# First token mix from row classes of the strided heads, wide strided loads, early buffers in late weights' places

## The chip, the core and the metric

The kernel runs on one core of one Trainium2 chip. The time is device microseconds for one execution, from inputs in DRAM to the output in DRAM. It is given as the median of several runs; beside it stands one profiled execution, whose trace is read here. The engines of the core: PE (TensorE, matmuls; PEld is its weight load), DVE (VectorE), ACT (ScalarE), POOL (GpSimd), SP (SyncE, which here issues nearly all DMAs).

## What is computed

```python
# attention: q, k, v are [8, 8, 576, 64], scale 1/8
mask_local   = (rel >= 0) & (rel < 32)                      # heads 0..3
mask_strided = (rel >= 0) & (pos_k % 32 == pos_q % 32)      # heads 4..7
attn = softmax(where(mask, scale * q @ k.T, -1e9)); x = concat_heads(attn @ v)   # x: [8, 576, 512]
# token mix of rank 32, then an MLP with a residual
u  = x + (x.transpose(0, 2, 1) @ U @ V).transpose(0, 2, 1)  # U: [576, 32], V: [32, 576]
out = u + relu(u @ w_ch1) @ w_ch2                           # w_ch1: [512, 2048], w_ch2: [2048, 512]
```

The inputs U, V, w_ch1 and w_ch2 arrive as 64-bit floats, all others as 32-bit.

## The kernel before

The rows of x are cut into tiles of 128 (four per batch, and one shared tail per pair of batches), two tiles to a block, 18 blocks. Each block runs 16 steps, one for each 128 columns of w_ch1: GEMM1 (L706, 12 matmuls 128x256 into ph) gives h^T, ACT writes relu(h) rounded (gh, L710), DVE what is left of it (gl, L711), and GEMM2 (L723, 6 matmuls 128x512) adds to the block's accumulator. Three products (high by high, low by high, high by low) stand for one product in full 32-bit precision. u^T of a block is held as uh and ul in the same sense. Blocks 0 and 1 run interleaved, block 1 two steps behind.

The weights come as 32 chunks of 128x512 64-bit numbers, 512 KB each, in the order group g = 0..3, then w1 (i = 0) or w2 (i = 1), then t = 0..3; chunk number 8g + 4i + t. A chunk is loaded raw (L150) and turned into a rounded high and a low part in the same place: ACT takes the absolute value of the upper words into a buffer cv (L110, Abs), DVE shifts and joins three times (L112, L113, L115), ACT casts the high part (L168), POOL subtracts for the low part (L169). There are three cv buffers; one is held from Abs to the end of L169. Step fc of block 0 or 1 needs w1 chunks of its group g = fc // 4.

The strided heads of batches 0 and 1 run on PE (early_strided): k and q are read with 18 rows a head and 32 positions to a row (tile kq), transposed (L343), scored (L356), softmaxed in s_str, multiplied with v (tile sv, L388) into two halves o_str, and these go through DRAM (tile od) into the layout of x (tile xg; L401). Strided heads of the other batches run on POOL and DVE. Local heads (early_local and its blocks) run on PE, with vt as the values. The token mix of batch 0 first makes t = x^T U (mix_t_first, L553 to L567), then adds V^T t to x in place (mix_u, L576 to L584) and transposes blocks 0 and 1 in the middle of it (transposes, L671 to L676).

The program is written as generators that are drawn in a loop (first_attention, then the loop over steps); a scheduler then fixes the order on each engine. CONV0, CONVE say from which draw on, and how often, a chunk is converted before the steps begin; LD0, LDR when weights are loaded; B1S when batch 1's attention begins. SP's queue issues its DMAs in program order, and an issue waits until the eighth one before it has landed. The q loads of batch 0 go through ACT's queue.

Of the kernel before, what the change touches and what calls it, by code (L numbers as in the profile page):

```python
# [7 lines left out]
F32 = mybir.dt.float32  # L8
# [27 lines left out]

@with_exitstack
def fused_kernel(ctx, tc, q, k, v, U, V, w1_in, w2_in, masks, eye, out):
# [48 lines left out]

    last_dma = [None]

# [13 lines left out]
    def to_f32(raw, p, n):  # L103


        rv = raw.bitcast(I32).rearrange("p (n two) -> p n two", two=2)
        lo_w, hi_w = rv[:, 0:n, 0], rv[:, 0:n, 1]
        cv = cvt("cv")
        f = cv[0:p, 0:n]
        nc.scalar.activation(out=f, in_=hi_w.bitcast(F32), func=AF.Abs, scale=2.0 ** -112)  # L110
        i = cv.bitcast(I32)[0:p, 0:n]
        nc.vector.tensor_scalar(out=i, in0=i, scalar1=3, scalar2=None, op0=ALU.logical_shift_left)  # L112
        nc.vector.scalar_tensor_tensor(out=i, in0=hi_w, scalar=-0x80000000, in1=i,  # L113
                                       op0=ALU.bitwise_and, op1=ALU.bitwise_or)
        nc.vector.scalar_tensor_tensor(out=i, in0=lo_w, scalar=29, in1=i,  # L115
                                       op0=ALU.logical_shift_right, op1=ALU.bitwise_or)
        return f

    def small_weights():
# [197 lines left out]
    def early_strided(b, eng=None):  # L317


        tb = 64 * (b % 2)  # L320
        quarters = [slice(32 * h, 32 * h + NCH) for h in range(4)]
        kq = [[ubuf([128, 1024], "kq") for _ in range(2)] for _ in range(2)]
        for bufs in kq:
            for x, buf in enumerate(bufs):
                (nc.vector if b == 0 and x == 0 else nc.gpsimd).memset(buf, 0.0)
# [7 lines left out]
        for h in range(4):  # L333
            dma(out=sv[quarters[h]], in_=v[b, 4 + h].rearrange("(i r) d -> i (r d)", r=32))
        yield
# [24 lines left out]
        yield  # L360
        s_sb = ubuf([128, 1024], "s_str")
        nc.gpsimd.memset(s_sb, 0.0)
# [5 lines left out]
        yield  # L368
        nc.scalar.activation(out=sv4, in_=sv4, func=AF.Exp, scale=0.125)
        yield  # L370
# [7 lines left out]
        yield  # L378
        o_sb = [ubuf([128, 16, D], "o_str") for _ in range(2)]
        od = dp.tile([4, 32, 32, D], F32, name="od")  # L380
        nj = 4 * width
        for r0 in range(0, 32, 2 * nj):
# [14 lines left out]
            if r1 + 2 * nj == 16:  # L397
                dma(out=od.rearrange("h i r d -> (h i) r d")[:, 16 * half:16 * half + 16], in_=o_sb[half])
        yield
        xg, xt = x_tiles(b)  # L400
# [142 lines left out]

    def mix_t_first(b, tst):

        xg, xt = x_tiles(b)
        tb = 64 * (b % 2)
        ta = att([128, DM], "ta")
        for half in range(2):
            cs = slice(256 * half, 256 * half + 256)  # L550
            ps_a = psx1()[:, 0:256]
            for j in range(4):
                nc.tensor.matmul(ps_a[32 * j:32 * j + 32, :], U_sb[:, j, :], xg[:, j, cs], start=True, stop=False,  # L553
                                 skip_group_check=True, tile_position=(0, 32 * j))
            for j in range(4):
                part = slice(64 * j, 64 * j + 64)
                nc.tensor.matmul(ps_a[32 * j:32 * j + 32, part], U_sb[tb:tb + 64, 4, :],
                                 xt[tb:tb + 64, 256 * half + 64 * j:256 * half + 64 * j + 64], start=False, stop=True,
                                 skip_group_check=True, tile_position=(tb, 32 * j))
            nc.scalar.copy(out=ta[:, cs], in_=ps_a)  # L560
        yield
        st = psx2()
        for half in range(2):
            cs = slice(256 * half, 256 * half + 256)
            nc.tensor.matmul(st[0:96, half, 0:256], fold, ta[:, cs], start=True, stop=True)
            nc.scalar.copy(out=tst[:, cs], in_=st[0:96, half, 0:256])
            nc.vector.tensor_tensor(out=tst[32:64, cs], in0=st[32:64, half, 0:256], in1=tst[32:64, cs].bitcast(F32), op=ALU.subtract)  # L567
        yield

    def mix_u(b, tst):  # L570
        xg, xt = x_tiles(b)
        tb = 64 * (b % 2)
        for t in (0, 2):
            pv = psx2()
            for s in range(2):
                nc.tensor.matmul(pv[:, s, :], Vst[:, 128 * (t + s):128 * (t + s) + 128], tst, start=True, stop=True)  # L576
# [3 lines left out]
            if b == 0 and t < 2 * NLEAD:  # L580
                yield from transposes(t // 2)
        pv = psx1()
        nc.tensor.matmul(pv[0:tb + 64], Vst[:, 512 - tb:576], tst, start=True, stop=True)
        nc.vector.tensor_tensor(out=xt[tb:tb + 64, :], in0=pv[tb:tb + 64, :], in1=xt[tb:tb + 64, :], op=ALU.add)  # L584
        yield
# [12 lines left out]
    def mixed(b, halves_):  # L598
        tst = att([96, DM], "tst", F32R)
        if b == 0:  # L600
            yield from mix_t_first(b, tst)
        else:
            for half in halves_:
                yield from mix_t(b, tst, half)
        yield from mix_u(b, tst)

    def first_attention():
# [14 lines left out]
        sw = small_weights()  # L622
        next(sw)
        yield
# [4 lines left out]
        yield from mixed(b, (0, 1))  # L629

# [13 lines left out]

    vt0 = const.tile([128, 1184], F32, name="vt0")
    fold = ap_.tile([128, 336], F32, name="s_st", tag="s_st")[:, 0:96]

# [11 lines left out]
    def transposes(n):  # L659
# [5 lines left out]
        if n < N_PE_T:  # L665
            uh, ul = parts()
            pts = psx2()
            for s, tid in enumerate(blocks[n]):
                x = tile_src(tid)
                for dc in range(NDC):  # L670
                    nc.tensor.transpose(out=pts[:, s, 128 * dc:128 * dc + 128], in_=x[:, 128 * dc:128 * dc + 128],  # L671
                                        identity=ident)
                src = pts[:, s, :].rearrange("p (d a x) -> p d a x", d=NDC, x=32)
# [7 lines left out]
        for s, tid in enumerate(blocks[n]):  # L681
            x = tile_src(tid)
            nc.vector.transpose(out=bt[:, :, s].rearrange("p q d x -> p d q x"),
                                in_=x.rearrange("p (d q y) -> p d q y", q=4, y=32))
            yield
# [12 lines left out]
    def gemm1(n, fc):  # L698
# [10 lines left out]
        gl = mp.tile([128, 256], F32R, name="gl", bufs=3)  # L709
        nc.scalar.activation(out=gh[:, 0:W], in_=ph[:, 0:W], func=AF.Relu)  # L710
        nc.vector.scalar_tensor_tensor(out=gl[:, 0:W], in0=ph[:, 0:W], scalar=0.0, in1=gh[:, 0:W].bitcast(F32),  # L711
# [47 lines left out]
    for i, _ in enumerate(first_attention()):  # L759
        load_ahead(int((i - LD0) * LDR))  # L760
        if i >= CONV0 and i % CONVE == 0:
            convert(counts["conv"] + 1)
# [8 lines left out]
    sgen, sb, free = None, NSP, False  # L771
    tr = None
    seq = sorted(((n, fc) for n in range(NLEAD) for fc in range(NFC)), key=lambda z: (z[1] + SKEW * z[0], z[0]))
    seq += [(n, fc) for n in range(NLEAD, len(blocks)) for fc in range(NFC)]
    lead_t = seq.index((0, NFC - 1)) if NLEAD > 1 else NFC - 6
    for step, (n, fc) in enumerate(seq):
# [15 lines left out]
        if nb < B and step >= window[nb][0]:  # L792
# [5 lines left out]
            while done < want:  # L798
# [66 lines left out]
```

## Time and profile before

| | |
|---|---|
| median of 3 runs | 1039.06 us (1036.94 to 1039.64) |
| profiled execution | 1040.9 us |
| its span in the trace | 1039.0 us |
| mean granted clock of PE | 0.959 |
| DMA, whole span | 72.06 MB, mean 69 GB/s |

The span is what the trace covers; the profiled execution's time holds 1.9 us more. A page of the profile gives busy time by engine and groups of instructions; windows cut the span by time. How a row reads: start, length, engine, line, operation, output and inputs, shapes, count, and in brackets how long the engine was idle before it and what released it.

### The profile page before, as it was taken

The page shows a single profiled execution, that of the slowest core. Times are in us where ns is not written, and L with a number is a line of the kernel's source. Part 1 is how long each engine was busy: PE and PEld are TensorE (multiplying, and loading weights), DVE is VectorE, ACT ScalarE, POOL GpSimd, SP SyncE. Part 2 cuts the span into 40 slices and gives each one's busy share as a digit, 9 for nine tenths or more (in the row PEclk, how much of TensorE's full clock was granted, in tenths as well). Part 3 has the DMA queues.
Part 4 walks back from the last instruction along what each step waited for, and adds up shares of the span by engine and source line. Part 5 has one row for each costly group of instructions (what it writes and reads, how often), then busy time and mean ns, then how long its engine had stood idle before and what let it go on. Part 6 is the DMA issues. An engine that isn't in the chain of part 4 may idle for free.

```text
span 1039.0 us, 21886 instructions
## 1 busy us (share of the span) xinstructions
PE 966.9 (93%) x9056; PEld 832.6 (80%) x9056; DVE 610.7 (59%) x1117; ACT 273.2 (26%) x635; POOL 360.3 (35%) x389
## 2 busy tenths in 40 slices
PE   4535788999999999999999999999999999999997
PEld 3424576888888888888888888888888888999996
DVE  1727798577767674761657875786587754222121
ACT  2414454212421242111332133213321332211110
POOL 2122254645284434640319341944194400000000
PEclk9556799999999999999999999999999999999999
DMA  6576742414323224131240434043404300101000
GB/s 147 145 163 170 254 190 45 74 48 83 60 53 69 62 47 66 27 81 39 49 73 19 88 64 89 4 95 57 87 10 94 53 21 13 50 1 41 1 21 21
DMA packets 182571, 72.06 MB, mean 69 GB/s; under 512 B 156856, under 2 KB 172504, under 8 KB 182328
## 3 DMA queue, kind: packets, MB, share of 16 engines
q1 hardware_dynamic: 181056, 69.78, 29.4%
q8 instruction: 71, 1.16, 0.5%
q10 hardware_dynamic: 1416, 0.89, 0.3%
q14 instruction: 28, 0.23, 0.1%
HBM read 51.22 MB, written 11.53 MB: 60 GB/s over the span
## 4 chain that ended last, share of the span: by engine, by line
PE 83%; DVE 7%; DMA 6%; issue 2%; SPq 2%; ACT 0%; DVEq 0%; ACTq 0%
PE ph L706 38%; PE acc L723 36%; DMA raw<-in_moe_w_ch_dram 3%; DVE cv L115 2%; SPq L94 2%; PE px L723 1%; PE px L223 1%; DVE cv L113 1%; DVE st L498 1%; PE px L255 1%; PE px L527 1%; PE px L243 1%; DMA kq<-in_k_dram 1%; PE px L576 1%; PE px L531 1%
## 5 line engine op out<-in xcount | busy, mean ns | idle before, releaser
L706 PE MATMUL ph<-uh,w 128*128 128x256 f32 x2304 | 468.3, 286 | 7.4 <-DVE gl L711 7.4
L706 PEld LDWEIGHTS ph<-uh,w 128*128 128x128 f32 x2304 | 375.1, 189 | 25.3 <-DVE gl L711 11.1
L723 PE MATMUL acc<-w,gh 128*128 128x512 f32 x1088 | 350.6, 401 | 5.5 <-ACT gh L710 5.4
L706 PE MATMUL ph<-ul,w 128*128 128x256 f32 x1152 | 326.1, 283 | 0.0
L711 DVE SCALAR_TENSOR_TENSOR gl<-ph,gh 128x256 fp32r<-128x256 f32 x288 | 121.0, 420 | 289.3 <-ACT gh L710 288.1
L710 ACT ACTIVATE gh<-ph 128x256 fp32r<-128x256 f32 x288 | 110.1, 383 | 520.0 <-PE ph L706 470.9
L706 PEld LDWEIGHTS ph<-ul,w 128*128 128x128 f32 x1152 | 218.2, 189 | 10.5
L723 PEld LDWEIGHTS acc<-w,gh 128*128 128x128 f32 x1088 | 193.5, 189 | 39.8 <-ACT gh L710 5.6
L723 PE MATMUL acc<-w,gl 128*128 128x512 f32 x544 | 215.8, 397 | 0.0
L468 POOL TENSOR_TENSOR tmp<-st 128x576 f32<-128x576 f32 (+6 forms) x162 | 166.9, 1067 | 133.9 <-DMA vt<-in_v_dram 85.5
L496 POOL TENSOR_TENSOR tmp<-st,s_st 128x448 f32<-128x448 f32 (+7 forms) x162 | 136.1, 869 | 214.2 <-DVE st L498 84.4
L498 DVE TENSOR_REDUCE st<-tmp 128x64 f32<-128x64 f32 (+8 forms) x162 | 135.9, 866 | 2.5 <-POOL tmp L496 1.7
L723 PEld LDWEIGHTS acc<-w,gl 128*128 128x128 f32 x544 | 102.4, 188 | 20.5
L470 DVE TENSOR_REDUCE s_st<-tmp 128x9 f32<-128x576 f32 (+6 forms) x162 | 87.5, 563 | 15.7 <-POOL tmp L468 15.6
L169 POOL TENSOR_TENSOR w<-cv,w 128x512 fp32r<-128x512 f32 x32 | 44.9, 1406 | 119.9 <-ACT w L168 119.9
L112 DVE TENSOR_SCALAR cv<-cv 128x512 int32<-128x512 int32 (+3 forms) x35 | 23.3, 667 | 51.7 <-ACT cv L110 51.6
L513 ACT COPY xg<-st 32x256 f32<-32x256 f32 x96 | 38.8, 404 | 23.5 <-DVE st L498 22.5
L115 DVE SCALAR_TENSOR_TENSOR cv<-raw,cv 128x512 int32<-128x512 int32 x32 | 34.0, 1063 | 0.5
L110 ACT ACTIVATE cv<-raw 128x512 f32<-128x512 f32 x32 | 21.8, 680 | 36.4 <-DMA raw<-in_moe_w_ch_dram 27.7
L693 DVE TENSOR_TENSOR ul<-u,uh 128x1024 fp32r<-128x1024 f32 x15 | 18.4, 1229 | 20.6 <-ACT uh L692 14.7
L168 ACT CAST w<-cv 128x512 fp32r<-128x512 f32 x32 | 19.9, 621 | 33.3 <-DVE cv L115 29.3
L343 PE MATMUL ph<-ident,kq 128*128 128x128 f32 x64 | 15.0, 398 | 14.0 <-DMA kq<-in_k_dram 9.8
(127 smaller groups left out, 603.5 us busy)
## 6 DMA issues: line engine op xcount, KB each, us to landing
raw<-in_moe_w_ch_dram SPq DMA_DIRECT2D x32, 512.0 KB
out_dram<-xg SPq DMA_DIRECT2D x32, 256.0 KB
u<-bt SPq DMA_DIRECT2D x240, 32.0 KB
vt<-in_v_dram SPq DMA_DIRECT2D x32, 144.0 KB
vt<-in_v_dram SPq DMA_DIRECT2D x32, 136.0 KB
st<-in_q_dram SPq DMA_DIRECT2D x24, 144.0 KB
st<-in_k_dram SPq DMA_DIRECT2D x24, 144.0 KB
st<-in_v_dram SPq DMA_DIRECT2D x24, 144.0 KB
```

The source lines that it names most:

```text
L112: nc.vector.tensor_scalar(out=i, in0=i, scalar1=3, scalar2=None, op0=ALU.logical_shift_left)
L115: nc.vector.scalar_tensor_tensor(out=i, in0=lo_w, scalar=29, in1=i, op0=ALU.logical_shift_right, op1=ALU.bitwise_or)
L169: nc.gpsimd.tensor_tensor(out=lo, in0=f, in1=hi.bitcast(F32), op=ALU.subtract)
L468: nc.gpsimd.tensor_tensor(out=tmp[:, 0:n], in0=sk[:, j0:j0 + n], in1=sq[:, i:i + 1].broadcast_to([128, n, D]), op=ALU.mult)
L470: late.append(lambda tmp=tmp, n=n, i=i, j0=j0: nc.vector.tensor_reduce(out=s_st[:, i, j0:j0 + n], in_=tmp[:, 0:n], axis=AX.X, op=ALU.add))
L496: nc.gpsimd.tensor_tensor(out=tv, in0=sv[:, 0:i + 1, d0:d0 + step], in1=s_st[:, i, 0:i + 1].broadcast_to([128, i + 1, step]), op=ALU.mult)
L498: late.append(lambda tv=tv, i=i, d0=d0, step=step: nc.vector.tensor_reduce(out=o_st[:, i, d0:d0 + step], in_=tv.rearrange("p j d -> p d j" ...
L513: nc.scalar.copy(out=xg[32 * i4:32 * i4 + 32, :, cs], in_=o_st[rows, i4:16:4, :])
L706: nc.tensor.matmul(ph[:, 0:W], w_parts[0, g, dc][:, part, fs], ut[:, :, :, dc, :], start=(dc == 0 and i == 0), stop=(dc == NDC - 1 and i = ...
L710: nc.scalar.activation(out=gh[:, 0:W], in_=ph[:, 0:W], func=AF.Relu)
L711: nc.vector.scalar_tensor_tensor(out=gl[:, 0:W], in0=ph[:, 0:W], scalar=0.0, in1=gh[:, 0:W].bitcast(F32), op0=ALU.max, op1=ALU.subtract)
L723: nc.tensor.matmul(accs[n][:, s, :], gt[:, cs], w_parts[1, g, f][:, part, :], start=(fc == 0 and i == 0), stop=(fc == NFC - 1 and i == 2))
```

## The change

**Loads.** k, q and v of the four strided heads come in one DMA each, from 32 rows a head instead of 18 (the last 14 rows of a head read into what follows it in memory and are not used); the memsets of kq go. The w1 chunks with t of 2 or 3 are loaded with rows permuted in the same manner.

**Places.** kq, s_str, o_str and three new tiles take the places of late weight chunks (28 to 31; 22 and 27; 20, 21 and 26, 24; 23 to 25) in place of the pool "u".

**First mix.** t of the strided half is made from o_str itself: U is written to DRAM (ud) and read back by row class (U_cls), 128 matmuls (32 classes, 4 heads) give its part of t, and u^T of blocks 0 and 1 is x^T, by matmuls with ident, plus t^T V in the same PSUM tile (first_u). mix_u of batch 0 follows behind step 4. The columns of the upper half of x are kept permuted, which splits a transpose or a product in two at several places.

**Conversions.** Abs (L112 of the changed kernel) is issued behind the exp of the strided heads, or behind the latest gh. Nine chunks are converted ahead of the steps, and batch 1's attention begins six draws later.

```diff
-LD0, LDR = 4, 0.5
+LD0, LDR = 8, 0.5
+MU0 = 4
-CONV0, CONVE = 12, 3
-B1S, B1E = 16, 1
+CONV0, CONVE, CONVP = 11, 1, 9
+B1S, B1E = 22, 1
...
-        nc.scalar.activation(out=f, in_=hi_w.bitcast(F32), func=AF.Abs, scale=2.0 ** -112)
+        with tc.issue_after(gate[0]) if gate else nullcontext():
+            nc.scalar.activation(out=f, in_=hi_w.bitcast(F32), func=AF.Abs, scale=2.0 ** -112)
...
+        ud = dp.tile([S, R], F32, name="ud")
+        dma(out=ud[0:512].rearrange("(t p) r -> p t r", p=128), in_=U_sb[:, 0:4])
+        dma(out=ud[512:576], in_=U_sb[0:64, 4])
+        for h in range(4):
+            dma(out=U_cls[32 * h:32 * h + NCH], in_=ud.rearrange("(i r) k -> i (r k)", r=32))
...
-                w1_in[128 * t:128 * t + 128, 512 * g:512 * g + 512]
+                w1_in[128 * t:128 * t + 128, 512 * g:512 * g + 512] if t < 2 else \
+                bass.AP(w1_in.tensor, w1_in[256 + 32 * (t - 2):, 512 * g:512 * g + 512].offset, [[64 * FF, 4], [FF, 32], [1, 512]])
...
+    def late(x, shape, name, dtype=F32):
+
+        i, g, t = chunks[x]
+        return const.tile(shape, dtype, name=name, tag=f"w{i}_{g}_{t}")
...
+        def wide(src, n, a):
+
+            return bass.AP(src.tensor, src[b, 4:5].offset + a, [[S * D, 4], [32 * D, 32], [1, n]])
+
+        kq = [[late(28 + 2 * x + y, [128, 1024], "kq") for y in range(2)] for x in range(2)]
...
-                for h in range(4):
-                    dma(out=bufs[half][quarters[h]],
-                        in_=src[b, 4 + h].rearrange("(i r) d -> i (r d)", r=32)[:, 1024 * half:1024 * half + 1024], eng=e)
+                dma(out=bufs[half], in_=wide(src, 1024, 1024 * half), eng=e)
...
-            dma(out=sv[quarters[h]], in_=v[b, 4 + h].rearrange("(i r) d -> i (r d)", r=32))
+        dma(out=sv, in_=wide(v, 32 * D, 0))
...
-        s_sb = ubuf([128, 1024], "s_str")
+        s_sb = late(22 if b == 0 else 27, [128, 1024], "s_str")
...
-        o_sb = [ubuf([128, 16, D], "o_str") for _ in range(2)]
+        o_sb = [late(x, [128, 16, D], "o_str") for x in ((20, 21) if b == 0 else (26, 24))]
...
+    def mix_first(tst):
...
+        for r in range(32):
+            for h in range(4):
+                rows = slice(32 * h, 32 * h + NCH)
+                nc.tensor.matmul(ps_b[32 * h:32 * h + 32], U_cls[rows, R * r:R * r + R], o_cls[r // 16][rows, r % 16],
+                                 start=r == 0, stop=r == 31, skip_group_check=True, tile_position=(32 * h, 32 * h))
...
+    def first_u(n, tst):
...
+        for d in range(4):
+            nc.tensor.matmul(pu[:, d // 2, 256 * (d % 2):256 * (d % 2) + 256], tst[:, 128 * d:128 * d + 128], Vst[:, 256 * n:256 * n + 256],
+                             start=False, stop=True, skip_group_check=True)
+        for a in range(2):
+            src = pu[:, a].rearrange("p (d s x) -> p d s x", d=2, x=32)
+            gate[:] = [nc.scalar.copy(out=uh[:, 2 * a:2 * a + 2], in_=src).ins]
+            nc.vector.tensor_tensor(out=ul[:, 2 * a:2 * a + 2], in0=src, in1=uh[:, 2 * a:2 * a + 2].bitcast(F32), op=ALU.subtract)
+        yield
...
+        yield from mix_first(tst0)
+        fu = [first_u(n, tst0) for n in range(NLEAD)]
...
+        if step >= MU0 and mu is not None and next(mu, "end") == "end":
+            mu = None
```

How the order on three engines moves. Line numbers of the changed kernel differ: L95 and L158 issue loads there, L183 is POOL's half of a conversion, L298 transposes xn, L781 is GEMM1, L798 GEMM2. SP's queue up to the first load of k for batch 1's local heads (xn; od is the DRAM copy of batch 0's strided output), before:

```order
L150 DMA raw_0_1_770<-in_moe_w_ch_dram 128x512
L94 DMA kq<-in_k_dram 18x1024 x4
L94 DMA kq<-in_q_dram 18x1024 x4
L94 DMA kq<-in_k_dram 18x1024 x4
L94 DMA kq<-in_q_dram 18x1024 x4
L94 DMA od<-o_str 128x1024
L94 DMA sv<-in_v_dram 18x2048 x4
L94 DMA xg<-od 128x4x64 x4
L94 DMA xt<-od 64x4x64
L150 DMA raw_0_2_808<-in_moe_w_ch_dram 128x512
L150 DMA raw_0_3_856<-in_moe_w_ch_dram 128x512
L94 DMA xn<-in_k_dram 128x4x64 x2
```

and now:

```order
L158 DMA raw_2_0_1092<-in_moe_w_ch_dram 128x512
L95 DMA xg<-od 128x4x64 x4
L95 DMA xt<-od 64x4x64
L158 DMA raw_2_0_835<-in_moe_w_ch_dram 128x512
L158 DMA raw_2_1_865<-in_moe_w_ch_dram 128x512
L158 DMA raw_2_2_1007<-in_moe_w_ch_dram 128x1x512
L158 DMA raw_2_1_1094<-in_moe_w_ch_dram 128x512
L158 DMA raw_3_1_1135<-in_moe_w_ch_dram 128x512
L158 DMA raw_2_3_1098<-in_moe_w_ch_dram 128x512
L158 DMA raw_3_0_1133<-in_moe_w_ch_dram 128x512
L158 DMA raw_3_0_1166<-in_moe_w_ch_dram 128x512
L95 DMA xn<-in_k_dram 128x4x64
```

Before, 8 of the 32 weight chunks stood ahead of xn on this queue; now 29 do (a row with 128x1x512 is one of the loads with permuted rows), and the copies of od.

PE's queue where the seventh step begins, before (px and acc are accumulators of blocks 1 and 0, L388 the strided heads of batch 1):

```order
L706 MATMUL ph<-uh,w_0_2_815 128x256
L706 MATMUL ph<-uh,w_0_3_876 128x256
L706 MATMUL ph<-ul,w_0_3_876 128x256
L706 MATMUL ph<-uh,w_0_3_876 128x256
L723 MATMUL px<-w_0_0_944,gl 128x512
L723 MATMUL px<-w_0_0_944,gh 128x512 x2
L723 MATMUL px<-w_0_0_944,gl 128x512
L723 MATMUL acc<-w_0_3_1394,gh 128x512 x2
L388 MATMUL px<-sv,PT_str 32x64 x5
```

and now:

```order
L781 MATMUL ph<-uh,w_0_3_724 128x256
L781 MATMUL ph<-ul,w_0_3_724 128x256
L781 MATMUL ph<-uh,w_0_3_724 128x256
L798 MATMUL acc<-w_0_3_842,gh 128x512 x2
L298 MATMUL px<-ident,xn 128x128 x4
L632 MATMUL px<-tst,Vst 128x256
L633 MATMUL px<-tst,Vst 128x256
L632 MATMUL px<-tst,Vst 128x256
L633 MATMUL px<-tst,Vst 128x256
L781 MATMUL ph<-uh,w_1_0_850 128x256
```

Behind six steps now stand transposes of xn, which holds k of batch 1's local heads, and behind them the products of mix_u of batch 0 (tst by Vst); before, both were done ahead of the first step.

POOL's queue at the end of the conversions, with the chunks' parts named w by group and place (the number behind them is the buffer's), before:

```order
L169 TENSOR_TENSOR w_2_2_1959<-cv,w_2_2_1959 128x512
L169 TENSOR_TENSOR w_2_3_1967<-cv,w_2_3_1967 128x512
L169 TENSOR_TENSOR w_3_0_2024<-cv,w_3_0_2024 128x512
L169 TENSOR_TENSOR w_3_1_2075<-cv,w_3_1_2075 128x512
L169 TENSOR_TENSOR w_3_2_2117<-cv,w_3_2_2117 128x512
L169 TENSOR_TENSOR w_3_3_2125<-cv,w_3_3_2125 128x512
L169 TENSOR_TENSOR w_3_0_2162<-cv,w_3_0_2162 128x512
L169 TENSOR_TENSOR w_3_1_2199<-cv,w_3_1_2199 128x512
L169 TENSOR_TENSOR w_3_2_2233<-cv,w_3_2_2233 128x512
L169 TENSOR_TENSOR w_3_3_2241<-cv,w_3_3_2241 128x512
```

and now:

```order
L183 TENSOR_TENSOR w_2_3_2047<-cv,w_2_3_2047 128x512
L183 TENSOR_TENSOR w_3_1_2096<-cv,w_3_1_2096 128x512
L373 MEMSET s_str 128x1024
L183 TENSOR_TENSOR w_3_3_2204<-cv,w_3_3_2204 128x512
L183 TENSOR_TENSOR w_3_0_2246<-cv,w_3_0_2246 128x512
L183 TENSOR_TENSOR w_3_1_2254<-cv,w_3_1_2254 128x512
L183 TENSOR_TENSOR w_3_2_2291<-cv,w_3_2_2291 128x512
L183 TENSOR_TENSOR w_3_3_2328<-cv,w_3_3_2328 128x512
L183 TENSOR_TENSOR w_3_2_2153<-cv,w_3_2_2153 128x512
L183 TENSOR_TENSOR w_3_0_2088<-cv,w_3_0_2088 128x512
```

Chunks 26 and 24 (w_3_2_2153 and w_3_0_2088), whose places o_str of batch 1 takes in between, are now finished last, behind chunks 28 to 31.

More of the change, by code (lines that the diff above doesn't have):

```diff
@@ L1 @@
-from contextlib import ExitStack
+from contextlib import ExitStack, nullcontext
 import concourse.bass as bass
@@ L368, in early_strided @@
         yield
[L369 removed]
+        exped = nc.scalar.activation(out=sv4, in_=sv4, func=AF.Exp, scale=0.125)
+        if b == 0:
+            gate[:] = [exped.ins]
         yield
@@ L563, in mix_t_first @@
         for half in range(2):
[L564 to L567, printed above, removed]
-        yield
+            nc.tensor.matmul(st[0:96, half, 0:256], fold, ta[:, 256 * half:256 * half + 256], start=True, stop=True)
@@ L570, in mix_u, with mix_product @@
+    def mix_product(out, cols, tst, permuted):
+        if not permuted:
+            nc.tensor.matmul(out, Vst[:, cols], tst, start=True, stop=True)
+            return
+        nc.tensor.matmul(out[:, 0:256], Vst[:, cols], tst[:, 0:256], start=True, stop=True)
+        nc.tensor.matmul(out[:, 256:512].rearrange("p (q d y) -> p q d y", d=2, y=32), Vst[:, cols],
+                         tst[:, 256:512].rearrange("p (d q y) -> p q d y", d=2, y=32), start=True, stop=True)
     def mix_u(b, tst):
@@ L575, in mix_u @@
             for s in range(2):
-                nc.tensor.matmul(pv[:, s, :], Vst[:, 128 * (t + s):128 * (t + s) + 128], tst, start=True, stop=True)
+                mix_product(pv[:, s, :], slice(128 * (t + s), 128 * (t + s) + 128), tst, b == 0)
             for s in range(2):
@@ L579, in mix_u @@
                 yield
-            if b == 0 and t < 2 * NLEAD:
-                yield from transposes(t // 2)
         pv = psx1()
-        nc.tensor.matmul(pv[0:tb + 64], Vst[:, 512 - tb:576], tst, start=True, stop=True)
+        mix_product(pv[0:tb + 64], slice(512 - tb, 576), tst, b == 0)
         nc.vector.tensor_tensor(out=xt[tb:tb + 64, :], in0=pv[tb:tb + 64, :], in1=xt[tb:tb + 64, :], op=ALU.add)
@@ L599, in mixed @@
         tst = att([96, DM], "tst", F32R)
[L600 to L604, printed above, removed]
+        for half in halves_:
+            yield from mix_t(b, tst, half)
         yield from mix_u(b, tst)
@@ L628, in first_attention @@
             yield
-        yield from mixed(b, (0, 1))
+        yield from mix_first(tst0)
+        fu = [first_u(n, tst0) for n in range(NLEAD)]
+        for g in fu:
+            next(g)
+        yield
+        for g in fu:
+            yield from g
     def attention(b):
@@ L645, in fused_kernel @@
     vt0 = const.tile([128, 1184], F32, name="vt0")
+    tst0 = att([96, DM], "tst", F32R)
+    U_cls = late(25, [128, 32 * R], "U_cls")
+    xT_str, o_cls = [], []
     fold = ap_.tile([128, 336], F32, name="s_st", tag="s_st")[:, 0:96]
```

89 lines of the change are left out of this document (59 added, 30 removed).

## The prediction

> **What bounds the kernel now.** I read the page first, then windows of the span, then the instructions of the windows in which TensorE waits.
>
> ```profile
> span 1039.0 us, 21886 instructions
> PE 966.9 (93%) x9056; PEld 832.6 (80%) x9056; DVE 610.7 (59%) x1117; ACT 273.2 (26%) x635; POOL 360.3 (35%) x389
> 113.08 0.39 PE L706 MATMUL ph<-uh,w 128*128 128x256 f32 x1
> 113.00:180.00 67.00, 52.54 (x549) 43.33 (x538) 61.47 (x87) 30.26 (x57) 29.06 (x20) 0.95 0.51 178
> 200.00:1039.00 839.00, 832.91 (x6851) 727.39 (x6850) 485.73 (x908) 200.90 (x494) 295.24 (x318) 1.00 0.24 49
> ...
> 113.00:136.00 23.00, 11.10 (x72) 10.37 (x72) 0.85 1.03 381
> 113.00:200.00 87.00, 38.80 (x264) 35.09 (x264) 0.96 0.53 164
> 113.00:1039.00 926.00, 470.02 (x3456) 452.11 (x3456) 0.99 0.27 60
> ```
>
> The window rows give length, busy time and count on PE (then PEld, DVE, ACT, POOL), the granted clock, the DMA share and GB/s; the last three count L706, GEMM1, alone. TensorE is busy for 93%, so the share says little about the change. By place: from 200 on PE is busy for 832.9 of 839 us, and there nothing but less matmul work could help. All that the change can move lies ahead of 200: GEMM1 starts at 113.1, and by 200 only 264 of its 3456 matmuls are issued, 22 steps of 12. What paces those 22 steps is the vector engine:
>
> ```profile
> L115 DVE SCALAR_TENSOR_TENSOR cv<-raw,cv 128x512 int32<-128x512 int32 x20 | 22.9, 1146 | 0.3
> L112 DVE TENSOR_SCALAR cv<-cv 128x512 int32<-128x512 int32 x20 | 17.1, 854 | 3.8 <-ACT cv L110 3.7
> L113 DVE SCALAR_TENSOR_TENSOR cv<-raw,cv 128x512 int32<-128x512 int32 x20 | 14.3, 717 | 0.1
> L711 DVE SCALAR_TENSOR_TENSOR gl<-ph,gh 128x256 fp32r<-128x256 f32 x13 | 5.3, 410 | 0.0
> L393 DVE TENSOR_TENSOR o_str<-px,rt_str 128x512 f32<-128x512 f32 x2 | 1.4, 676 | 0.0
> ...
> 188.56 1.44 PE ph L706 x12
> 191.40 1.44 PE ph L706 x12
> ```
>
> These groups are from 118 to 175. They sum to 61 us in 57, so DVE does not rest, and its records overlap a little: a weight chunk shows 0.854 + 0.717 + 1.146 = 2.72 us, but costs (57 - 5.3 - 1.4) / 20 = 2.5 of DVE's time; a gl costs 0.41. Behind the conversions PE sets the pace, at 191.40 - 188.56 = 2.84 us a step. So the time is about 200 us, at which 22 steps are done, plus 839. I forecast the moment R at which 22 steps are done in the changed kernel, and add the same 839.
>
> **The change, part by part.**
>
> The wide loads come first. Strided k, q and v, 18 rows a head and four heads, came as four DMAs; now one DMA reads four heads of 32 rows with a source pattern of [4][32][n] into 128 partitions. Late w1 chunks (t = 2, 3) get such a pattern too. That saves issues and moves 512 KB in place of 288. What counts is how many of the 16 DMA engines such a transfer uses. The ACT queue of before tells how it went with 18 rows:
>
> ```profile
> q10 hardware_dynamic: 1416, 0.89, 0.3%
> kq<-in_q_dram ACTq DMA_DIRECT2D x8, 72.0 KB
> xn<-in_q_dram ACTq DMA_DIRECT2D x2, 128.0 KB
> xn<-in_q_dram ACTq DMA_DIRECT2D x1, 32.0 KB
> ...
> 10.00:11.00 1.00, 1.00 (x7) 1.00 (x6) 0.00 (x0) 0.00 (x0) 0.00 (x0) 1.00 0.60 191
> 130.00:140.00 10.00, 9.39 (x69) 8.14 (x68) 9.92 (x13) 5.15 (x11) 5.57 (x4) 1.00 1.03 409
> ```
>
> The rows of data are 8 x 18 + 2 x 512 + 128 = 1296 packets; 120 are left, and 120 = 8 x 9 + 3 x 16: one closing write for each engine, if 18 rows are dealt to 9 engines and 128 or 64 to 16. The window at 10 us, full of 18-row loads from two queues, shows a share of 0.60, near 9/16, so it is the same engines each time. 18 is dealt in equal parts of its count, 9 x 2. If the count that is dealt is that of the outermost dimension, the new loads, outermost 4, get 4 engines. From the last row an engine moves 409 / 16 = 25.6 GB/s: 4 engines take 512 KB in 5.1 us, 1 MB (sv) in 10.2; 16 engines take 1.28 and 2.6. These are the two ends; no run here shows a nested source, so both stay. I take four engines: equal parts of the outermost count is what the one odd shape in the trace shows, though there outermost count and row count are the same 18.
>
> [...]
>
> SP's queue goes in order, at most eight transfers open, and a transfer on all 16 engines ends only when its parts behind the wide ones on the four engines do. So wide loads add up. Ahead of the load xn of batch 1 that PE's L298 (of the changed kernel) waits for, behind only six steps of GEMM1, stand: 8 kq and 8 w1 loads of 5.1 us and two sv of 10.2, 102 us; 21 whole chunks of 1.28, 27 us; about 5.2 MB of small ones at 409 GB/s, 13 us; the first transfer starts near 2 us. Sum 144 without gaps; issue waits (a lane, a buffer still in use, the U_cls loads behind the write of ud) make it 144 to 165, and I take 155. With 16 engines the wide ones take 25.6 in place of 102 and the load is not waited for.
>
> The first mix. Before, its start went through DRAM twice:
>
> ```profile
> 67.49 4.48 DMA od<-o_str
> 73.52 5.97 DMA xg<-od
> 79.74 1.08 PE L553 MATMUL ph<-xg,U_sb 128*32 128x256 f32 x8 [9.54 <-DMA xg<-od]
> 87.32 0.73 PE L576 MATMUL px<-tst,Vst 96*128 96x512 f32 x2 [0.98 <-DVE tst L567]
> 56.44 1.93 PE L388 MATMUL ph<-sv,PT_str 18*32 18x64 f32 x64 [1.70 <-DVE o_str L393]
> ```
>
> 10.5 us of transfers leave the path. In come 128 small matmuls (L584 of the changed kernel), by the last row 0.030 us each at half clock, 3.9 us, or half that warm; and u^T of blocks 0 and 1 is then finished in PSUM with some 3 us, where before transposes of 16 tiles were spread from 89 to 112. mix_u of batch 0 moves behind step 4: its five DVE additions of about 0.7, 3.4 us, lay on DVE before too, but earlier. What it waits for is the loads. Ahead of vt of the second pair of heads, which closes batch 0's attention, stand 12 wide loads of 5.1 and an sv, 71 us; 8 whole chunks, 10; about 3.2 MB of small ones, 8; with the start 92, with issue waits some 100. From there: the last products and divisions 5 us, then from the first U product to the first V product 87.3 - 79.7 = 7.6 as before, and u^T 3: first GEMM1 at 116, against 113.1. With 16 engines these loads end near 40 and bind nothing: the second half of o_str is there at 67.5 as before, and with about 8 for the mix GEMM1 starts at 76.
>
> Edits that I cost at nothing: the memsets of kq that go are POOL's, which nobody awaits there; the split transposes and the xs copies of later blocks fall behind 200, beside PE, with DVE busy 486 and ACT 201 of 839 us (without that cover, two operations of about 0.7 a tile would count).
>
> Conversions. Nine chunks instead of 12 stand ahead of the first GEMM1, so 19 chunks and 14 gl of DVE remain in the dense phase up to chunk 27, about 19 x 2.5 + 14 x 0.41 + 6 (the additions and the softmax of batch 1) = 59 us. DVE's order puts six chunks and six gl of it (18 us) ahead of the addition that waits for PE's queue behind L298: DVE is there at 116 + 18 = 134 and stands until 155. The rest is 12.7 x 2.5 + 8 x 0.41 + 4 = 39 us, to 194. Then six steps at PE's pace, 17 us: 211. The gate on Abs adds a wait on ACT, whose queue behind it holds the next gh; ACT is busy 30 of 67 us from 113 to 180, so I cost it at nothing; uncovered, it is at most one Abs a chunk.
>
> ```profile
> 64.26 0.67 ACT L110 ACTIVATE cv<-raw 128x512 f32<-128x512 f32 x1 [9.38 <-DMA raw<-in_moe_w_ch_dram]
> 66.62 0.69 DVE L115 SCALAR_TENSOR_TENSOR cv<-raw,cv 128x512 int32<-128x512 int32 x1
> 67.40 0.62 ACT L168 CAST w<-cv 128x512 fp32r<-128x512 f32 x1 [1.51 <-DVE cv L115]
> 68.10 1.27 POOL L169 TENSOR_TENSOR w<-cv,w 128x512 fp32r<-128x512 f32 x1 [7.01 <-ACT w L168]
> ```
>
> Late slots. o_str of batch 1 sits in the places of chunks 24 and 26. These two are on DVE before it, and each holds one of three cv buffers until o_str has left for DRAM. Chunks 28 to 31 then run one after another through one buffer: 64.26 to 69.37 is 5.1 us, 4.6 without a half microsecond in which DVE did other work; 18.4 for four. The last halves of o_str stand behind them on DVE. With nine more DVE operations of about 0.68 (two transposes, two additions, four o_str, one evacuation), 6 us, the write of od at 4.5, and the cast and POOL half of chunk 24 (0.62 + 1.27) the chain has 31 us, some 33 with hand-overs; step 23 (g = 3, chunk 24) waits for its end. It holds little dense work. Below, 9 us if the serial chunks fall away; above, 40.
>
> **Sum.** R = 155 + 39 + 17 + 33 = 244 against 200: +44, and 1.5 for half a mix of batch 1 that is left and a colder clock. Span 1039.0 + 45.5 = 1084.5; the profiled execution took 1040.9, 1.9 above its span, so 1086. The median of the runs, 1039.06, is 1.8 below the profiled one; that is left as it is, less than any bound here. The two uncertain terms (144 to 165; 33 between 25 and 40) give 1067 to 1104.
>
> **The rivals.**
>
> All 16 engines serve the wide loads: first GEMM1 at 76; DVE's 59 us run to 137 with a short wait; 17 us of steps, 154; the chain of 33, 187. R is 13 below 200, and 1.5 back: time 1029. From 1009 (chain 13 us) to 1042 (chain and hand-overs 46). This is the other side: the point is at R = 200, that is, if the wide loads cost together no more than some 55 us rather than 102 (each us above 25.6 delays R by about one once the queue binds, near 40). For it: 18-row loads cannot tell rows from outermost count. Against: equal parts of the outermost count fit.
>
> Four engines, but the late slots do not serialise (a cv buffer frees in time): chain 9 us, time 1086 - 24 = 1062. For it: the chain runs over five engines and my order of it may break at one. Against: three buffers and two holders stand in the order.
>
> The change does not do what it says: the u^T without a round trip is earlier only if loads allow; under four engines it is not, which is the forecast itself.
>
> **How the numbers follow.** Chances: forecast 0.62, late slots free 0.10, 16 engines 0.28. What a measurement of this kernel can tell from no change is about 0.3%, 3 us. Of the 16-engine case 0.20 is faster by more, 0.06 within, 0.02 slower; of the other two 0.01 within. Faster 0.20, same 0.07, slower 0.73. The range takes in the forecast's own 1067 to 1104, the 1062, and the upper part of the 16-engine case, from 1024; outside are 0.10 below and 0.05 above.
>
> **What would show it.** Right: kq loads at 5 us each, GB/s near 100 with a DMA share near 0.25 in the first 25 us; strided scores later than before; GEMM1 first near 116; PE and DVE idle together before a batch-1 load, ending near 155; a second idle stretch of PE that ends with L168 of chunk 24 near 243; PE full from there. Wrong: a share near 1.0 during kq, first GEMM1 before 85. If the first part is right and no stretch ends at chunk 24, the chain was misread.

## The result, and the profile after

| | before | changed |
|---|---|---|
| median | 1039.18 us (1036.94 to 1039.64, 4 runs) | 1129.95 us (1126.73 to 1134.4, 4 runs) |
| span of the profiled execution | 1039.0 us | 1128.9 us |

The ratio is 1.0881, 95% interval 1.0839 to 1.0923: the change makes the kernel 8.8% slower. Direction and first cause were forecast; the time lies 44 us above the 1086 forecast and above the range. The page of the changed kernel:

```profile
span 1128.9 us, 22425 instructions
PE 979.8 (87%) x9325; PEld 851.4 (75%) x9325; DVE 612.0 (54%) x1151; ACT 274.0 (24%) x638; POOL 359.2 (32%) x384
PEclk9755585995989999999999999999999999999999
DMA  3563655203232423231312423324340410111000
...
q10 hardware_dynamic: 1464, 1.34, 0.4%
```

PE is busy for 13 us more and the span is 90 us longer, so nearly all of the loss is waiting, in the first twelve of the 40 slices. The last row is ACT's load queue. Its data are 2 x 128 rows of kq, 2 x 512 and 128 of xn, 1408 packets; 56 of 4 bytes are left, and 56 = 2 x 4 + 3 x 16: each load of four heads was closed by four engines. The trace's semaphore events say the same load by load: each of the 18 loads of four heads or of permuted rows ends in four late updates, an 18-row load of before in nine, a whole chunk in 16. Windows while such loads run alone, and of a later stretch in which whole weight chunks and one chunk with permuted rows are under way together (columns as in the prediction):

```profile
11.00:15.00 4.00, 0.00 (x0) 0.00 (x0) 0.00 (x0) 0.00 (x0) 0.00 (x0) 1.00 0.26 105
132.00:137.00 5.00, 4.47 (x43) 4.07 (x43) 0.45 (x2) 0.40 (x2) 0.00 (x0) 0.50 0.27 97
172.00:178.00 6.00, 0.00 (x0) 0.00 (x0) 0.00 (x0) 0.00 (x0) 0.00 (x0) 0.50 1.03 214
```

A share of 0.26 at 105 GB/s (kq) and 0.27 at 97 (sv) is four engines of 16; at these rates 512 KB take 5.0 us and 1 MB 10.8, against 5.1 and 10.2 forecast. PE's rows where it waits:

```profile
118.31 0.39 PE L269 MATMUL px<-vt,PT 64*32 64x65 f32 x2 [22.25 <-DMA vt<-in_v_dram]
143.06 0.50 PE L781 MATMUL ph<-uh,w 128*128 128x256 f32 x2 [0.44 <-ACT uh L623]
189.16 1.09 PE L298 MATMUL px<-ident,xn 128*128 128x128 f32 x4 [30.14 <-DMA xn<-in_k_dram]
```

PE stands 22 us for the values of the second pair of heads, and GEMM1 begins at 143.1; then six steps; then 30 us of standing for k of batch 1, which lands at 189. A third stretch shows in the chain of waits, from the softmax transposes of batch 1's strided heads (L386) to step 23:

```profile
242.71 1.31 DVE PT_str L386 x2
244.04 0.63 ACT w L182
244.83 1.27 POOL w L183
...
279.23 3.16 DMA od<-o_str
282.47 0.63 ACT w L182
283.14 5.18 PE ph L781 x24
```

This too was forecast: chunks 28 to 31 pass one by one, od is written, and only then is chunk 24 cast and step 23 issued. How much of it costs time is another matter, as the windows of GEMM1 alone show, first of before, then of the changed kernel:

```profile
113.00:231.30 118.30, 55.10 (x384) 50.93 (x385) 0.97 0.42 129
231.30:1039.00 807.70, 414.91 (x3072) 401.18 (x3072) 1.00 0.24 50
```

```profile
143.00:190.50 47.50, 9.91 (x72) 9.23 (x72) 0.69 0.65 179
143.00:283.00 140.00, 37.17 (x264) 34.84 (x264) 0.80 0.35 93
143.00:320.20 177.20, 55.47 (x384) 52.67 (x384) 0.83 0.34 87
320.20:1128.90 808.70, 417.21 (x3072) 404.06 (x3072) 0.99 0.25 50
```

From step 33 on (384 matmuls done) both need the same, 807.7 and 808.7 us. Step 33 is the first of block 2, which needs u of batch 1. The whole loss lies before it: 320.2 against 231.3. So each experiment below is read by the start of a few steps, which are the starts of every twelfth GEMM1 matmul in its trace (e6 is left out, since its profiled execution was a disturbed one; the times of e6 and e15 below leave out one such execution each):

| run | step 1 | 7 | 19 | 23 | 33 | from 33 to the end |
|---|---|---|---|---|---|---|
| before | 113.1 | 138.4 | 188.4 | 201.0 | 231.4 | 807.6 |
| changed | 143.1 | 190.9 | 236.6 | 283.1 | 320.3 | 808.6 |
| e1 all cut | 96.9 | 117.8 | 165.1 | 211.0 | 247.2 | 809.2 |
| e2 kq, sv cut | 118.1 | 154.4 | 200.0 | 246.1 | 281.9 | 809.0 |
| e3 w1 cut | 131.2 | 160.5 | 206.2 | 252.8 | 289.9 | 808.6 |
| e4 own buffers | 144.2 | 191.9 | 243.2 | 256.7 | 315.2 | 808.3 |
| e7 18 rows | 92.4 | 121.3 | 168.0 | 216.7 | 252.9 | 809.4 |
| e8 cut, draw 16 | 102.2 | 117.8 | 165.6 | 213.0 | 250.9 | 807.9 |
| e9 e8 + buffers | 100.5 | 116.2 | 173.7 | 186.7 | 238.3 | 810.5 |
| e10 cut, buffers, draw 10 | 122.3 | 139.5 | 191.0 | 204.8 | 234.6 | 807.4 |
| e11 e9, steps 2 to 20 | 99.6 | 123.8 | 176.9 | 190.9 | 225.8 | 807.0 |
| e12 e10 with 18 rows | 122.9 | 138.6 | 190.0 | 205.2 | 234.7 | 806.7 |
| e13 wide on ACT's queue | 178.5 | 195.0 | 241.7 | 289.7 | 325.8 | 809.4 |
| e14 e11, wide again | 161.9 | 186.4 | 240.3 | 253.8 | 288.8 | 807.4 |
| e15 e11 with 18 rows | 106.7 | 131.3 | 185.3 | 198.9 | 233.9 | 808.3 |

### The profile page after: what moved, and what is told of

Its sections match the earlier page's. It is cut to its first block, busy times and chain, and to the rows that moved or that the text cites. A ratio compares the mean times of both kernels' runs of the same rounds, so it can differ in the third digit from the quotient of the medians.

```text
span 1128.9 us, 22425 instructions
## 1 busy us (share of the span) xinstructions
PE 979.8 (87%) x9325; PEld 851.4 (75%) x9325; DVE 612.0 (54%) x1151; ACT 274.0 (24%) x638; POOL 359.2 (32%) x384
## 4 chain that ended last, share of the span: by engine, by line
PE 77%; DMA 10%; SPq 5%; DVE 5%; issue 2%; ACT 1%; POOL 1%; DVEq 0%; POOLq 0%; ACTq 0%
PE ph L781 35%; PE acc L798 32%; SPq L95 5%; DMA xn<-in_k_dram 3%; DMA raw<-in_moe_w_ch_dram 3%; DMA vt<-in_v_dram 2%; DMA kq<-in_q_dram 2%; PE px L798 2%; PE px L237 1%; PE px L269 1%; PE px L257 1%; PE ph L584 1%; DVE st L518 1%; PE px L630 1%; PE px L547 1%
## 5 line engine op out<-in xcount | busy, mean ns | idle before, releaser
L781 PE MATMUL ph<-uh,w 128*128 128x256 f32 x2304 | 470.3, 287 | 5.4 <-ACT w L182 2.1
L781 PEld LDWEIGHTS ph<-uh,w 128*128 128x128 f32 x2304 | 378.1, 191 | 20.2 <-DVE gl L786 2.6
L798 PE MATMUL acc<-w,gh 128*128 128x512 f32 x1088 | 349.4, 400 | 0.8 <-ACT gh L785 0.8
L781 PE MATMUL ph<-ul,w 128*128 128x256 f32 x1152 | 328.1, 285 | 2.1 <-DVE ul L750 1.8
L786 DVE SCALAR_TENSOR_TENSOR gl<-ph,gh 128x256 fp32r<-128x256 f32 x288 | 120.9, 420 | 288.8 <-ACT gh L785 287.7
L781 PEld LDWEIGHTS ph<-ul,w 128*128 128x128 f32 x1152 | 220.2, 191 | 13.1 <-DVE ul L750 2.1
L798 PEld LDWEIGHTS acc<-w,gh 128*128 128x128 f32 x1088 | 193.3, 188 | 34.7 <-ACT gh L785 1.2
L798 PE MATMUL acc<-w,gl 128*128 128x512 f32 x544 | 215.6, 396 | 0.0
L488 POOL TENSOR_TENSOR tmp<-st 128x576 f32<-128x576 f32 (+6 forms) x162 | 169.3, 1081 | 123.8 <-DMA vt<-in_v_dram 104.1
L798 PEld LDWEIGHTS acc<-w,gl 128*128 128x128 f32 x544 | 102.2, 188 | 20.3
L183 POOL TENSOR_TENSOR w<-cv,w 128x512 fp32r<-128x512 f32 x32 | 45.4, 1424 | 192.2 <-ACT w L182 188.0
L269 PE MATMUL px<-vt,PT 64*32 64x65 f32 x1152 | 18.3, 241 | 34.1 <-DMA vt<-in_v_dram 33.3
L298 PE MATMUL px<-ident,xn 128*128 128x128 f32 (+1 forms) x40 | 8.9, 353 | 41.0 <-DMA xn<-in_k_dram 41.0
L269 PEld LDWEIGHTS px<-vt,PT 64*32 64x32 f32 x1152 | 14.6, 113 | 39.7 <-issue 37.2
L298 PEld LDWEIGHTS px<-ident,xn 128*128 128x128 f32 (+1 forms) x40 | 6.7, 187 | 43.6 <-issue 43.2
L644 DVE TENSOR_TENSOR xg<-px,xg 128x512 f32<-128x512 f32 x32 | 20.4, 683 | 30.7 <-PE px L633 28.4
L114 DVE TENSOR_SCALAR cv<-cv 128x512 int32<-128x512 int32 (+3 forms) x35 | 20.1, 577 | 25.5 <-ACT cv L112 25.1
```

Of the source, the lines that this page charges most:

```text
L183: nc.gpsimd.tensor_tensor(out=lo, in0=f, in1=hi.bitcast(F32), op=ALU.subtract)
L269: nc.tensor.matmul(op[32 * o4:32 * o4 + 32, hh, (D + 1) * t:(D + 1) * t + D + 1], PT[rows, 32 * c:32 * c + 32], vt[rows, c], start=True, s ...
L488: nc.gpsimd.tensor_tensor(out=tmp[:, 0:n], in0=sk[:, j0:j0 + n], in1=sq[:, i:i + 1].broadcast_to([128, n, D]), op=ALU.mult)
L781: nc.tensor.matmul(ph[:, 0:W], w_parts[0, g, dc][:, part, fs], ut[:, :, :, dc, :], start=(dc == 0 and i == 0), stop=(dc == NDC - 1 and i = ...
L798: nc.tensor.matmul(accs[n][:, s, :], gt[:, cs], w_parts[1, g, f][:, part, :], start=(fc == 0 and i == 0), stop=(fc == NFC - 1 and i == 2))
```

## The experiments

Every run is of the changed kernel with an edit, unless it says otherwise; ratios are against runs of the kernel before on the same chip (1039.6 to 1040.0 us).

**The engines (e1, e2, e3).** e1 cuts each load from four heads, or of permuted rows, into four of 32 rows; e2 does so for kq and sv alone, e3 for w1 alone.

```diff
-                dma(out=bufs[half], in_=wide(src, 1024, 1024 * half), eng=e)
+                for h in range(4):
+                    dma(out=bufs[half][32 * h:32 * h + 32], in_=wide(src, 1024, 1024 * half, h), eng=e)
...
+                    for h in range(4):
+                        nc.sync.dma_start(out=raws[i, g, t][32 * h:32 * h + 32],
+                                          in_=w1_in[256 + 32 * (t - 2) + 64 * h:256 + 32 * (t - 2) + 64 * h + 32, 512 * g:512 * g + 512])
```

> The changed kernel with each load of four heads (kq, sv, permuted w1 chunks) cut into four loads of 32 rows; everything else is as in the change. Theory (four engines): a source whose outermost count is 4 is dealt to 4 DMA engines, so cutting it gives 16 engines back. First GEMM1 from 143 to 70-85, DMA share near 1.0 while kq loads, no stand of PE before the batch-1 xn of over 10 us; the second stand (chunk 24) stays at 25-40 us; time 1025-1045. Rival (queue order): not the engines but the order and the eight open transfers of the load queue delay the loads; then first GEMM1 stays above 120 and the time above 1090, since 48 loads more stand on that queue.

> Only kq and sv are cut in four; the eight permuted w1 chunks stay whole. Theory (four engines): of the 102 us of wide transfers ahead of the batch-1 xn, 61 go; first GEMM1 90-110, time 1055-1090. Rival (queue order): as the changed kernel or slower, 1125-1150.

> Only the permuted w1 chunks are cut in four; kq and sv stay whole. Theory (four engines): 41 of the 102 us go, half of them ahead of the first GEMM1; first GEMM1 near 125, time 1080-1105. Rival (queue order): 1125-1150. If kq and sv alone were the cause (they come first), the time would stay near 1130 too, but with the second run near 1040.

e1: 1058.1 us, ratio 1.0175 (1.0153 to 1.0197). e2: 1092.49, 1.0506 (1.0487 to 1.0525). e3: 1099.06, 1.0571 (1.0546 to 1.0595). The same bytes in more loads take 72 us off, so the rival of the queue's order falls. The parts take off 37.5 and 30.9, together 68 of 72. But e1 missed its own expectation, 1025 to 1045, and first GEMM1 came at 96.9, not 70 to 85; e2, too, lies just above its range, and its first GEMM1, 118.1, above 90 to 110. Windows of e1 show at what rate the loads went:

```profile
5.00:10.00 5.00, 1.94 (x8) 1.57 (x8) 0.00 (x0) 0.00 (x0) 1.67 (x9) 1.00 1.03 229
70.00:74.00 4.00, 2.97 (x115) 2.38 (x116) 3.86 (x11) 1.22 (x2) 1.23 (x1) 0.50 1.02 405
```

While cut loads run (5 to 10), all engines are busy and move 229 GB/s; whole chunks of 128 rows (70 to 74) move 405. A load of 32 rows writes into 32 of the 128 partitions; that this sets the rate is not shown here.

**The kernel before with wide loads (e6).** Its kq and sv in single loads (the memsets of kq fall away with that), nothing else of the change.

```diff
-                for h in range(4):
-                    dma(out=bufs[half][quarters[h]],
-                        in_=src[b, 4 + h].rearrange("(i r) d -> i (r d)", r=32)[:, 1024 * half:1024 * half + 1024], eng=e)
+                dma(out=bufs[half], in_=wide(src, 1024, 1024 * half), eng=e)
...
-        for h in range(4):
-            dma(out=sv[quarters[h]], in_=v[b, 4 + h].rearrange("(i r) d -> i (r d)", r=32))
+        dma(out=sv, in_=wide(v, 32 * D, 0))
```

> The kernel before, with nothing of the change but the single loads of four heads for kq and sv (w1 chunks and all else as before). Theory (four engines): eight kq and two sv, 61 us on four engines, two thirds of it ahead of the first GEMM1 or of batch 1's scores; first GEMM1 125-145 instead of 113, time 1055-1085. Rival (only the changed order of the program makes the wide loads costly): 1036-1043.

1080.77 us, ratio 1.0402 (1.0382 to 1.0423): 41 us lost by these loads alone. Four engines are costly in the old order as in the new.

**The late places (e4).**

```diff
-        s_sb = late(22 if b == 0 else 27, [128, 1024], "s_str")
+        s_sb = late(22, [128, 1024], "s_str") if b == 0 else ubuf([128, 1024], "s_str")
...
-        o_sb = [late(x, [128, 16, D], "o_str") for x in ((20, 21) if b == 0 else (26, 24))]
+        o_sb = [late(x, [128, 16, D], "o_str") for x in (20, 21)] if b == 0 else [ubuf([128, 16, D], "o_str") for _ in range(2)]
```

> The changed kernel with s_str and o_str of batch 1 in buffers of their own again instead of the places of chunks 27, 26 and 24; loads stay wide. Theory (late places serialise the last conversions): the stand of PE from 243 to 283 shrinks to the 10-15 us of attention work, time 1095-1110, first GEMM1 unchanged at 143. Rival (the stand is batch 1's attention chain itself, late because batch 1 starts late): time 1120-1132.

1125.27 us, ratio 1.0822 (1.0804 to 1.084): the time is the rival's, and the gain on the changed kernel, 4.7 us, is hardly more than the spread of its runs. Step 23 does come 26 us earlier (256.7), so the places did hold it; but step 33 only 5 us (315.2). The wait moved from step 23 to step 33. Its chain ahead of step 33:

```profile
298.68 1.08 DVE tst L561
299.90 1.20 PE px L630 x2
...
305.48 5.36 DVE s_st L490 x11
...
312.05 0.59 ACT uh L749
...
316.50 3.57 PE ph L781 x15
```

t of batch 1 (tst) is ready at 299.8, then come its mix (L630) and the transposes of block 2, with work for batch 2 (s_st) ahead of them on DVE. u of batch 1 is what is late.

**The bytes of the loads (e7).** kq and sv in 18 rows with the rest of the tile zeroed, as before; w1 cut in four (the cut shown is against e1; sv likewise).

```diff
-                    dma(out=bufs[half][32 * h:32 * h + 32], in_=wide(src, 1024, 1024 * half, h), eng=e)
+                    dma(out=bufs[half][32 * h:32 * h + NCH],
+                        in_=src[b, 4 + h].rearrange("(i r) d -> i (r d)", r=32)[:, 1024 * half:1024 * half + 1024], eng=e)
```

> The changed kernel with kq and sv read as before (18 rows a head, the rest of the tile set to zero) and the permuted w1 chunks cut in four. Theory (loads of 32 rows cut in four still write 32 partitions each and run at 200-235 GB/s at a full share, and they carry 32 / 18 of the bytes): first GEMM1 from 97 to 80-88, time 1043-1052. Rival (the bytes do not matter, latency and issue do): first GEMM1 95-100, time 1055-1062.

1061.45 us, ratio 1.0211 (1.019 to 1.0231), first GEMM1 at 92.4. The theory missed, and the time lies in the rival's range: GEMM1 begins 4.5 us earlier than in e1, between the two ranges, and nothing of it reaches step 33.

**The start of batch 1 (e8 to e12).** Draw 16 in place of 22 (e8), with s_str and o_str of batch 1 in own buffers (e9), draw 10 (e10), or the remaining draws over steps 2 to 20 in place of 29 (e11); e12 is e10 with 18 rows.

```diff
-B1S, B1E = 22, 1
+B1S, B1E = 16, 1
...
-W0, W1 = 2, 29
+W0, W1 = 2, 20
```

> All wide loads cut in four, and batch 1's attention begun at draw 16 as in the kernel before, instead of 22. Theory (from step 33 on every kernel so far needs the same 808 to 809 us, and step 33 waits for u of batch 1, so the late start of batch 1 is what is left of the loss): step 33 from 247 to 225-238, time 1034-1047. Rival (the late places hold step 23 at 205-211 whatever batch 1 does): time 1052-1060.

> As the run before it, and s_str and o_str of batch 1 in buffers of their own. Theory (batch 1's chain first, late places second): step 33 at 215-228, time 1024-1037, at or below the kernel before. Rival (the four-fold loads at half rate are what remains): time 1040-1056.

> Wide loads cut in four, s_str and o_str of batch 1 in buffers of their own, batch 1's attention begun at draw 10: its last matmuls with v now stand behind step 13 instead of step 25, its mix behind 24 instead of 32. Theory (what is left of the loss is u of batch 1, for which step 33 waits): no stand ahead of step 33, step 33 at 212-226, time 1020-1035. Rival (the work of batch 1 only moves ahead of the steps and takes as long there): first GEMM1 later by what is gained, step 33 at 230-240, time 1039-1050.

> As e9, and batch 1's remaining draws are spread over steps 2 to 20 instead of 2 to 29: mix behind steps 23 to 28 instead of 32. Theory (u of batch 1): step 33 from 238 to 220-230, time 1028-1040. Rival (work only moves): step 33 at 234-242, time 1044-1052.

> As e10 with kq and sv read in 18 rows a head, as in the kernel before. In the changed order 18 rows gained nothing (1061 against 1058). Theory (the loads no longer bind once they run on 9 or 16 engines): within 5 us of e10. Rival (their bytes bind now that batch 1's loads come earlier): 6-15 us faster than e10.

e8: 1060.45 us, 1.0194 (1.0179 to 1.021), step 33 at 250.9: the rival, half a us above its range. As long as the places hold, batch 1's last products stand behind step 22 all the same. e9: 1051.95, 1.0117 (1.0095 to 1.0138): both together gain 6 us on e1, and the time lies in the rival's range; step 31 is at 214.2, 11 us ahead of before, and then 24 us pass to step 33. e10: 1044.41, 1.0048 (1.0033 to 1.0063): the rival again; an early batch 1 puts the first GEMM1 off from 100 to 122, and step 33 stands at 234.6. e11: 1036.99, 0.9973 (0.9961 to 0.9984): step 33 at 225.8, within the theory's range; its windows of GEMM1:

```profile
99.00:225.70 126.70, 54.23 (x384) 50.63 (x384) 0.97 0.36 95
225.70:1032.90 807.20, 415.28 (x3072) 401.34 (x3072) 1.00 0.24 49
```

It is the one version that is faster than the kernel before, by 0.27%. e12: 1042.03, 1.0025 (1.0016 to 1.0034), 2.4 us from e10: the bytes of the loads do not bind there.

**Another queue, and whether the losses add (e13 to e15).**

```diff
-                nc.sync.dma_start(out=raws[i, g, t], in_=src)
+                (nc.scalar if i == 0 and t >= 2 else nc.sync).dma_start(out=raws[i, g, t], in_=src)
```

and eng=nc.scalar for kq and sv (e13); e11 with the loads whole again (e14) or in 18 rows (e15).

> The changed kernel with every wide load (kq, sv, permuted w1 chunks) issued on ACT's queue, all other loads on SP's as they are; loads stay whole, on four engines by the theory. Theory A (small loads stand behind the wide ones on one queue of eight open transfers, which adds 34-45 us of gaps to the 144): first GEMM1 from 143 to 110-125, batch-1 xn from 189 to 120-150, time 1085-1110. Theory B (the four engines themselves are the whole price): the wide loads still end near 105-140, first GEMM1 135-145, time 1115-1132.

> As e11 (buffers of their own for s_str and o_str of batch 1, batch 1 from draw 16 on and over steps 2 to 20), but with the loads wide again. If the two losses add up: e11 plus the 70 us that the cut brought in the changed kernel, 1095-1115. If the wide loads hid the second loss: no better than the changed kernel with its buffers, 1118-1130.

> As e11, with kq and sv read in 18 rows a head. If the bytes of the 32-row loads still cost: 1028-1034. If not: within 4 us of e11, 1033-1041.

e13: 1136.81 us, 1.0927 (1.0911 to 1.0942), above both theories: no stand for xn, but first GEMM1 at 178.5. A window of it while batch 0's attention waits for loads:

```profile
60.00:105.00 45.00, 11.23 (x422) 8.56 (x422) 7.81 (x17) 5.52 (x13) 0.00 (x0) 0.50 0.31 117
```

The share of 0.31 is that of the wide loads with little beside them. Of SP's queue, the view of waits says why (what waited, for what, us in all, how often, the longest):

```profile
SPq L158 <- DMA kq<-in_k_dram: 41.9, 1, 41.9
```

From 60.4 to 102.6 SP's queue issues nothing. The semaphores of the eight open transfers go round over both queues together (in the trace of the changed kernel eight of them serve all 605 DMAs of SP's and ACT's queues), and the next chunk on SP's queue waits for the one that a kq load of ACT's queue holds until it lands at 102.6. So the small loads were still behind the wide ones, through this wait: the first values of batch 0's local heads land at 126.9, in the changed kernel at 80.9. What a queue with open transfers of its own would bring, no run shows. e14: 1098.73, 1.0567 (1.0554 to 1.0581), 61.7 us above e11: the losses add, nearly. e15: 1041.75, 1.0017 (1.0004 to 1.0029), 5 us above e11 and 1 above its range; no gain from fewer bytes.

## Why the forecast was right in its cause and too small

**Four engines: right.** The closing writes (56 = 2 x 4 + 3 x 16), the four late semaphore updates, the share of 0.26, the 5.0 us a load where it runs alone, and four pairs of runs: 72 us between the changed kernel and e1, 62 between e14 and e11, 41 between e6 and before, 37.5 for kq and sv alone.

**The load queue: this term failed.** The prediction put "issue waits ... make it 144 to 165, and I take 155" and "first GEMM1 at 116"; measured 189 and 143.1. The order of the queue was right: a whole chunk issued at 49.6 has twelve of its 16 updates by 55.8 and the last four from 71.4 to 72.1, behind two wide loads that land at 63.8 and 70.9. The sizes were not, since each load was priced as if it ran alone. The semaphore events give the landing of each load. If each is charged with the time since the landing before it, then up to xn the 16 wide loads of 512 KB come to 99 us, where the sum had 82; the two sv to 28, for 20; the whole chunks (one more than was counted) to 36, for 27; all else, with the start, to 26, for 15. That is 45 us more than the sum of 144, and the forecast had 11 of them, as issue waits. Most of it is in the wide loads themselves. Where kq loads run with little beside them, they land 5.0 and 5.3 us apart (at 94.0, 99.1 and 104.4), as forecast; beside whole chunks on the other engines a wide load took 10.5, 7.2 and 9.5 us. The last of these stands in the chain of waits ahead of xn (start, length from issue to landing):

```profile
165.41 15.11 DMA raw<-in_moe_w_ch_dram
180.53 8.49 DMA xn<-in_k_dram
...
189.16 1.09 PE px L298 x4
```

This is the chunk with permuted rows. The chunk ahead of it lands at 171.0, it lands at 180.5, and only then is the second load of xn, the eighth issue behind it, let go. The window 172 to 178 above lies in this stretch: 214 GB/s at a full share. That is an account by landings, not an experiment, and e13 does not settle it; why loads on four and on 16 engines went slower together than alone stays open.

The first GEMM1 was late for a second reason. The values it waits for came at 118 to 121, not at some 100; but from the first U product (123.2) to GEMM1 (143.1) 19.8 us also passed, where the forecast had 7.6 + 3. The 128 small matmuls leave 256 records in the trace and took 7.8 us, not 3.9: the 0.030 us was that of a record, and each of these matmuls leaves two. The sum does not feel this, since PE then stands for xn.

**The work from 189 to L386: right in length, in part by luck.** 39 + 17 = 56 us forecast, 242.7 - 189 = 54 measured. But DVE was to set the pace of the first 39; in these 53.7 us PE was busy for 51.0 and DVE for 39.6.

**The late places: mechanism right, its worth wrong.** The chain of 33 took 283.1 - 242.7 = 40 us. But the prediction took it as the thing that sets R, and added "the same 839" behind it. e4 removes it and gains 4.7 us (between e8 and e9 it is 8.5), since step 33 waits for u of batch 1 in any case; the rival "late slots free", at 1062 or 24 us less, was priced by the same error. What is the same behind every order is the time from step 33, 806.7 to 810.5 us in all traces of the table, not that from step 23 (845.7 here, 838.0 before). Behind R that is 5 us more than the 839 + 1.5 of the forecast.

**The sum.** xn landed 34 us later than forecast, the stretch to L386 took 2 less, the chain 7 more, and the time from step 23 on was 5 longer: 44 in all, from 1086 to 1130.

**The rival of 16 engines, at 1029**, can be held against e1: 1058. First GEMM1 came at 96.9 instead of 76. The last products with v, for o_str, end near 74.6, where that rival had 67.5, and the mix and u^T took 22 us from there, where it had 8; the half rate of the 32-row loads bears on the first part; that it bears on the second no row shows, and e7, with fewer bytes, gained 4.5 us in all. Then 46 us from step 19 to 23 (165.1 to 211.0) where the places hold and batch 1 is still to do. At step 19 e1 is 23 us ahead of before (165.1 against 188.4), but work of batch 1 that stood ahead of the first step before is then still to be done; how much of the 23 us the first u^T without the round trip brought was not separated from that. e10 against e11 shows that the place of this work decides what is left: too early it delays step 1, too late step 33.

## What to carry to other kernels

Look at the outermost count of the source before joining loads into one: here a load that covers 128 partitions ran on four engines where that count was 4 (a share of 0.26, 105 GB/s), and what stood behind it on its queue waited with it (xn until 189 us). A price taken from loads that run alone was too low here for loads that run beside others. To price a change near the start, find the step from which all versions need the same time, and ask what that step waits for; a wait removed ahead of it may only move. Work that is put off to start a bounding stage sooner is still due before the first step that needs its result.

## What the runs showed of the hardware

Loads of 32 rows into 32 partitions moved 229 GB/s at a share of 1.03, against 405 for loads of 128 rows, both on 16 engines (e1). No run varies the partitions alone, so the reason is not shown. And loads on four engines and on 16 went slower together than alone: in the changed kernel from 172 to 178, with a chunk of permuted rows and whole chunks under way together, 214 GB/s at a share of 1.03, and packets of 4 KB took 314 ns in the mean; in the kernel before from 130 to 140, with whole chunks alone, 409 GB/s at 1.03, and 163 ns. So the share alone does not tell that the engines move what they can.
